# Column sums in four parts, paced weight splits and later value halves in a clustered attention with an MLP behind it

## The chip, the cores and the metric

The kernel runs on one core of one Trainium2 chip. Its time is device microseconds (us) of one execution. The engines are named as in the profile: PE (TensorE, the matmuls), DVE (VectorE), ACT (ScalarE), POOL (GpSimd), and SP, whose queue issues every DMA of this program.

## The reference: clustered attention, then an MLP

Four batches of eight heads, 768 positions, 64 numbers a head. Queries and keys are each assigned to the nearest of 16 centroids of their head; a query sees only the keys of its own cluster. Behind it comes an MLP on the 3072 rows of 512 numbers.

```python
mask = q_assign[:, :, :, None] == k_assign[:, :, None, :]
scores = scale * np.matmul(q, k.transpose(0, 1, 3, 2))
scores = np.where(mask, scores, -1000000000.0)
attn = np.exp(scores - np.max(scores, axis=-1, keepdims=True))
attn = attn / (np.sum(attn, axis=-1, keepdims=True) + 1e-09)
x = np.matmul(attn, v)            # heads side by side: [3072, 512]
h = x @ w_in                      # 512 -> 2048
r = np.maximum(h, 0.0)
g = s * (r * r) + b
out = g @ w_out                   # 2048 -> 512
```

The constant b is added to every element of g, so it reaches the output as b times the column sums of `w_out`. These column sums are one of the things that the change moves.

## The kernel before: units of attention, steps of the MLP, one loop

**Units and steps.** The work is one loop over i (lines 802 to 845). Attention is cut into 192 units: a unit is one head with 128 queries, and in step i unit i gets its scores (`scores`, line 507, four matmuls), its maximum (`maxima`, line 521, DVE) and its exponentials (`exps`, line 528, ACT). The transposed probabilities meet the values four steps later (`value`, line 605, 18 matmuls into the unused columns of a scores bank; the first 16 units go another way, `values`, line 572). Four units make a piece of x (`finish_x`, line 631). The MLP runs `LAG` = 21 steps behind: step m = i - 21 does one of 16 slices ft of the hidden width for 256 rows: `mlp_in` (line 670, 12 matmuls), `mlp_relu` (line 679, three operations on ACT), `mlp_gl` (line 689, POOL), and three steps later `mlp_out` (line 694, 12 matmuls). After the sixteenth slice the two accumulators are scaled, the bias is added (line 711, DVE) and the result is stored.

**Precision.** Most operands are kept as two float16 tiles, a high half (ACT copies the scaled number to float16) and a low half (DVE takes the scaled number minus the high half). `split` (line 216) does this for keys, queries and values, `wsplit` (line 300) for the weights: per slice ft one ACT and one DVE operation for `w_in` (tiles `wis`) and one of each for `w_out` (`wos`). The operation on DVE is a SCALAR_TENSOR_TENSOR with two inputs, line 225 or 310.

**Weights.** The weights arrive as 64 bit floats in 32 DMAs, are packed into float32 by ACT and DVE (`rebase`, `narrow`, lines 242 to 250) and their magnitudes are taken (`bound`, line 252). Only when all 32 are known is the scale in `glob` known (`finish_w_in`, `finish_w_out`), and only then can any weight be split. `wsplit(ft)` is registered at step 17 + ft (line 742). The slices from 4 on are issued behind `first_x`, the two operations that end the fourth piece of x (lines 639 to 641, 306 and 309): from that point nothing holds them back.

**Value halves.** `prep_v(0)` (line 451) splits the four value tiles of the first batch. The first units don't use the halves, only units from 16 on do. It asks for steps 14, 16, 18 and 20 (line 482), but the order of instructions on each engine is not the order of this text: a scheduler orders them by their priority and by when it takes their inputs to be ready. `issue_after`, used through `behind` (line 149), tells it to put an instruction behind another. Nothing of the kind stands at line 490.

**Column sums.** `column_sums` (line 314) is called once, with the last slice of the first MLP chunk (line 709): 32 matmuls with a matrix of ones over all the `wos` halves into one bank, `pb`, and one scaling by DVE into `bias` (line 321).

**Banks.** `small_bank` (line 102) hands out two PSUM banks, h and m, in turn, from step 21 on: the hidden slices of the MLP, the small reductions and `pb` share them.

Of the kernel before, what the change touches and what calls it, by code (L numbers as in the profile page):

```python
# [13 lines left out]
AF = mybir.ActivationFunctionType  # L14
ALU = mybir.AluOpType
# [11 lines left out]
def tile_cluster_attention_mlp(ctx, tc, q, k, v, cent, w_in, w_out, s_in, b_in, out):  # L27
# [47 lines left out]
    last_transpose = [None]  # L75
    first_x = [None, None]
    last_turn = [None]
# [60 lines left out]
    def copy(eng, dst, src):  # L138
        if eng is A:
            A.activation(dst, src, AF.Copy)  # L140
        else:
            eng.tensor_copy(dst, src)

# [156 lines left out]
    def wsplit(ft):  # L300
        while narrowed[0] < 2 * NF:
            next(wgen)
        made = []
        for w, f in ((wi[ft], glob[:, 2:3]), (wo[ft], glob[:, 5:6])):
            e = parts(weight_tile(f"w{'io'[len(made)]}s{ft}"))
            with behind(*first_x[: 2 * (ft >= 4)]):
                A.activation(e[:, 0], w, AF.Copy, scale=f)
            yield
            with behind(*first_x[: 2 * (ft >= 4)]):
                V.scalar_tensor_tensor(e[:, 1], w, f, e[:, 0], op0=ALU.mult, op1=ALU.subtract)  # L310
            made.append(e)
        WSP[ft] = (made[0], made[1].rearrange("p e a f -> p e (a f)"))

    def column_sums():
        pb = small_bank("pb", "m")
        for ft in range(NF):
            for e in range(2):
                nc.tensor.matmul(pb, ones16, WSP[ft][1][:, e, :], start=(ft + e == 0), stop=(ft + e == NF))
        V.tensor_tensor(glob[:, 7:8], bv, glob[:, 4:5], op=ALU.mult)
        bias.append(weight_tile("bias").rearrange("p a f -> p (a f)"))  # L320
        V.tensor_scalar(bias[0], pb, glob[:, 7:8], None, op0=ALU.mult)

# [69 lines left out]
    def prep_q(b, c, hq):  # L392
        n = f"{b}_{c}_{hq}"
        nh = 4
        if b or c > 1:
            qn = sb.tile([P, CT * DM], F32, tag="stage", name=f"qn_{n}", bufs=3)
        else:
            qn = sb.tile([P, T * P], F32, tag="big", name=f"qn_{n}", bufs=BIGN)
# [52 lines left out]
    def prep_v(b):  # L451
# [28 lines left out]
        for hp in range(NP):  # L480
            if b == 0:
                yield from until(RAW - 2 + 2 * hp)
            if b == 1 and hp == 0:
# [5 lines left out]
            G.memset(vh[:, :, :, D:], 1.0)  # L489
            yield from split(vh[:, :, :, :D], vl, vns[hp], vm[:, 7:8], False)  # L490
            if hp < NP - 1:
# [56 lines left out]
    def low(i):  # L548
        u = U[i]
        if i < TURN:  # L550
# [7 lines left out]
            for e in range(2):  # L558
# [3 lines left out]
                if i < RAW:  # L562
                    copy((V, A)[e], flat[:, cols], turned[:, e, : n * P])
                else:
                    A.activation(two[:, 0, cols], turned[:, e, : n * P], AF.Copy)
                    V.tensor_tensor(two[:, 1, cols], turned[:, e, : n * P], two[:, 0, cols], op=ALU.subtract)
# [64 lines left out]
    def finish_x(g):  # L631
# [6 lines left out]
        xn = sb.tile([P, CT, 2, 2, D], F16, tag="xn", name=f"xn_{g}", bufs=1)  # L638
        made = [A.activation(xn[:, :, 0], xs, AF.Copy), absmax(XM[(b, c)][:, hp : hp + 1], xs.rearrange("p t h d -> p (t h d)"))]
        if g == NP - 1:  # L640
            first_x[:] = made
        yield
# [36 lines left out]
    def mlp_relu(b, c, ft):  # L679
        n = f"{b}_{c}_{ft}"  # L680
        ph = GS[(b, c, ft)]
        r = sb.tile([P, CW], F32, tag="r", name=f"r_{n}", bufs=2)
        A.activation(r, ph[:, :CW], AF.Relu, scale=MS[(b, c)][0])  # L683
        g = gs[:, ft % 4]
# [9 lines left out]
    def mlp_out(b, c, ft):  # L694
# [10 lines left out]
        if ft == NF - 1:  # L705
            _, e, acc = MS.pop((b, c))
            o = sb.tile([P, CT, DM], F32, tag="stage", name=f"o_{n}", bufs=3)
            if b + c == 0:
                column_sums()
            for t in range(CT):  # L710
# [30 lines left out]
    for ft in range(NF):  # L741
        at(LAG - 4 + ft, wsplit(ft))
    wgen = weights()

# [127 lines left out]
```

## Time and profile before

| | us |
|---|---|
| median of 3 runs | 911.07 |
| lowest and highest of the runs | 909.8 and 915.86 |
| the profiled execution, its own time | 912.4 |
| its span | 910.7 |
| PE busy in the span | 830.3 (91%) |
| ACT busy | 712.7 (78%) |
| DVE busy | 631.2 (69%) |
| POOL busy | 544.0 (60%) |

An execution's own time and its span differ by 1.7 us, what lies around the program. Busy shares are averages over stages that differ much, so the prediction reads them by stretches of the span. In a group's row the columns are: line, engine, operation, output<-input, count, then busy us and mean ns of one. In the timeline a row gives the start, the duration and, in brackets, how long the engine stood idle ahead of it and what ended that. A row of a table by stretches gives the stretch, its length, for each engine the busy us with the number of instructions, the granted TensorE clock as a share of full speed, and the share and rate of the DMA.

### The profile page before, as it was taken

How to read it: one execution, taken by the hardware profiler on the slowest of the kernel's cores; microseconds unless marked ns; L12 is line 12 of the kernel's file. 1: busy time of each engine (PE TensorE's matmuls, PEld its weight loads, DVE VectorE, ACT ScalarE, POOL GpSimd, SP SyncE). 2: the span in 40 equal slices, each digit the busy share in tenths (PEclk: the TensorE clock that was granted, in tenths of full speed). 3: DMA queues.
4: the chain of work that ended last, by engine and by line, in shares of the span. 5: the costliest groups of instructions: out<-in, count | busy, mean ns of one | idle time of the engine just before them, and what ended most of it. 6: DMA issues, size and time to landing. Idle time of an engine off the chain costs nothing.

```text
span 910.7 us, 22840 instructions
## 1 busy us (share of the span) xinstructions
PE 830.3 (91%) x8625; PEld 591.9 (65%) x8625; DVE 631.2 (69%) x1673; ACT 712.7 (78%) x1406; POOL 544.0 (60%) x580
## 2 busy tenths in 40 slices
PE   1675786899999899999999999999999999999997
PEld 0564664566677667777667767677677777777764
DVE  8789789979778758766877667669777557564200
ACT  4579786867798779889888788988988788788553
POOL 3111024587687668768778667777876667676422
PEclk9977576999999999999999999999999999999999
DMA  5997624697998897989899989689988767676200
GB/s 151 245 287 239 205 49 91 163 178 163 182 181 140 182 209 139 175 158 180 175 180 190 181 152 185 154 150 207 177 156 171 140 124 173 117 149 132 59 24 23
DMA packets 437758, 144.23 MB, mean 158 GB/s; under 512 B 405392, under 2 KB 434064, under 8 KB 437648
## 3 DMA queue, kind: packets, MB, share of 16 engines
q1 hardware_dynamic: 437648, 142.78, 76.1%
q8 instruction: 67, 1.10, 0.5%
q14 instruction: 43, 0.35, 0.1%
HBM read 35.69 MB, written 6.29 MB: 46 GB/s over the span
## 4 chain that ended last, share of the span: by engine, by line
PE 44%; DVE 21%; DMA 14%; ACT 9%; issue 6%; POOL 3%; SPq 2%; DVEq 0%; ACTq 0%; POOLq 0%
PE h L676 15%; PE acc L703 14%; PE sc L516 7%; DMA kn<-in_k_dram 4%; DVE ssm L526 4%; DMA qn<-in_q_dram 4%; ACT p L536 2%; PE sc L617 2%; PE sc L619 2%; ACT ssm L533 2%; PE sc L618 2%; DMA vn<-in_v_dram 2%; DVE ka L225 2%; SPq L570 1%; POOL ph L568 1%
## 5 line engine op out<-in xcount | busy, mean ns | idle before, releaser
L568 POOL TENSOR_TENSOR ph<-p,ph 128x768 f16<-128x768 f32 x176 | 296.3, 1683 | 154.0 <-ACT ph L140 63.9
L676 PE MATMUL h<-xk,wis 128*128 128x256 f16 x2304 | 288.3, 274 | 5.1 <-DMA xk<-xn 2.3
L703 PE MATMUL acc<-wos,gs 128*128 128x512 f16 x1152 | 280.6, 379 | 2.0 <-DVE o L711 0.8
L676 PEld LDWEIGHTS <-wis 128*128 128x128 f16 x2304 | 222.9, 98 | 63.6 <-issue 6.3
L536 ACT ACTIVATE p<-sc,ssm,qsm 128x768 f32<-128x768 f32 x192 | 189.3, 986 | 4.3
L526 DVE TENSOR_REDUCE ssm<-sc 128x1 f32<-128x768 f32 x192 | 181.9, 947 | 6.3 <-PE sc L516 6.2
L691 POOL TENSOR_TENSOR gs<-r,gs 128x256 f16<-128x256 f32 x192 | 136.1, 710 | 64.3 <-ACT r L686 55.3
L703 PEld LDWEIGHTS <-gs 128*128 128x128 f16 x1152 | 104.4, 98 | 94.8 <-issue 1.1
L533 ACT ACTIVATE ssm<-ssm,lift,qsm 128x1 f32<-128x1 f32 x192 | 73.0, 381 | 83.2 <-DVE ssm L526 82.5
L140 ACT ACTIVATE ph<-p 128x768 f16<-128x768 f32 x164 | 137.2, 836 | 0.6
L683 ACT ACTIVATE r<-h,cf 128x256 f32<-128x256 f32 x192 | 89.1, 465 | 39.8 <-PE h L676 34.0
L617 PE MATMUL sc<-halves,PT 128*128 128x65 f16 x1032 | 113.0, 195 | 0.1
L618 PE MATMUL sc<-halves,PT 128*128 128x64 f16 x1032 | 112.9, 192 | 0.0
L619 PE MATMUL sc<-halves,PT 128*128 128x65 f16 x1032 | 112.6, 193 | 0.0
L516 PE MATMUL sc<-keys,QA 128*128 128x384 f16 x384 | 99.8, 341 | 12.8 <-ACT p L536 10.9
L516 PE MATMUL sc<-keys,QB 128*128 128x384 f16 x384 | 99.7, 341 | 8.3 <-DMA QB<-qb 8.3
L617 PEld LDWEIGHTS <-PT 128*128 128x128 f16 x1056 | 99.0, 97 | 11.9 <-DMA PT<-ph 0.8
L618 PEld LDWEIGHTS <-PT 128*128 128x128 f16 x1056 | 98.1, 99 | 11.6 <-issue 0.7
L619 PEld LDWEIGHTS <-PT 128*128 128x128 f16 x1056 | 98.3, 97 | 0.0
L686 ACT ACTIVATE r<-r 128x256 f32<-128x256 f32 x192 | 79.2, 413 | 4.0
L623 DVE TENSOR_SCALAR ssm<-sc 128x1 f32<-128x1 f32 x172 | 26.3, 153 | 80.5 <-PE sc L619 79.0
L685 ACT ACTIVATE gs<-r 128x256 f16<-128x256 f32 x192 | 78.6, 411 | 1.6
(191 smaller groups left out, 1104.7 us busy)
## 6 DMA issues: line engine op xcount, KB each, us to landing
wst<-in_moe_w_in_dram SPq DMA_DIRECT2D x16, 512.0 KB, 4.7
kn<-in_k_dram SPq DMA_DIRECT2D x16, 384.0 KB, 4.2
qn<-in_q_dram SPq DMA_DIRECT2D x24, 256.0 KB, 3.6
vn<-in_v_dram SPq DMA_DIRECT2D x16, 384.0 KB, 3.9
out_dram<-o SPq DMA_DIRECT2D x12, 512.0 KB, 3.3
wst<-in_moe_w_out_dram SPq DMA_DIRECT2D x8, 512.0 KB, 5.0
gs<-in_moe_w_out_dram SPq DMA_DIRECT2D x8, 512.0 KB, 5.8
PT<-ph SPq DMA_TRANSPOSE x176, 3.5
```

What stands on the lines that cost most here:

```text
L140: A.activation(dst, src, AF.Copy)
L516: last_score[0] = nc.tensor.matmul(sc[:, e, :HALF], X[:, col, :], y[:, h * S + e * HALF : h * S + (e + 1) * HALF], start=st, stop=not st)
L526: last_max[0] = V.tensor_reduce(SM[i // 4][:, 0, j : j + 1], U[i]["sc"], axis=AX.XY, op=ALU.max, negate=True)
L533: A.activation(bi, sm[:, 0, j : j + 1], AF.Identity, scale=u["scale"], bias=lift)
L536: last_exp[0] = A.activation(p.rearrange("p (a b) -> p a b", a=2), u["sc"], AF.Exp, bias=bi, scale=u["scale"], **total)
L568: G.tensor_tensor(u["ph"][:, 1, :], u["p"], u["ph"][:, 0, :], op=ALU.subtract)
L617: nc.tensor.matmul(o1, PT[:, kt, :], vh[:, h, kt, : D + 1], start=(kt == 0), stop=False)
L618: nc.tensor.matmul(o, PT[:, kt, :], vl[:, h, kt, :], start=False, stop=False)
L619: nc.tensor.matmul(o1, PT[:, T + kt, :], vh[:, h, kt, : D + 1], start=False, stop=(kt == T - 1))
L676: nc.tensor.matmul(ph[:, :CW], WSP[ft][0][:, wl, kt, :], XS[(b, c, kt)][:, :, xl, :], start=(i == 0), stop=(i == len(terms) - 1))
L691: G.tensor_tensor(g[:, 1, :], r, g[:, 0, :], op=ALU.subtract)
L703: nc.tensor.matmul(acc[:, t, :], g[:, gl, rows], WSP[ft][1][:, wl, :], start=(ft == 0 and gl + wl == 0), stop=(ft == NF - 1 and gl == 1))
```

## The change

Four edits.

1. `column_sums(n)` takes a quarter of the slices, waits until their `wsplit` has been issued, and runs from step 20 + 4n on. Each quarter has a bank of its own (`pb_0` to `pb_3`); the first writes `bias`, the others add to it with a SCALAR_TENSOR_TENSOR on DVE.
2. `wsplit(ft)`: ACT's part of the slices from 4 on is issued behind the newest `Relu` of the MLP, DVE's part behind the newest maximum; slices 1 to 3 behind the last copies of the first 16 units.
3. `prep_v(0)` asks for steps 16, 19, 22 and 25, and both operations of each split are issued behind the newest exponential and the newest maximum.
4. The query tile of chunk 1, second half of the first batch, comes from the three `stage` buffers, which the weights also use, and not from the eleven `big` ones.

```diff
-            with behind(*first_x[: 2 * (ft >= 4)]):
+            with behind(*([last_relu[0]] if ft >= 4 else last_copy if ft else ())):
                 A.activation(e[:, 0], w, AF.Copy, scale=f)
             yield
-            with behind(*first_x[: 2 * (ft >= 4)]):
+            with behind(*([last_max[0]] if ft >= 4 else last_copy if ft else ())):
                 V.scalar_tensor_tensor(e[:, 1], w, f, e[:, 0], op0=ALU.mult, op1=ALU.subtract)
...
-    def column_sums():
-        pb = small_bank("pb", "m")
-        for ft in range(NF):
+    def column_sums(n):
+        q = NF // 4
+        while len(WSP) < (n + 1) * q:
+            yield
+        pb = small_bank(f"pb_{n}", "h")
+        for ft in range(n * q, (n + 1) * q):
             for e in range(2):
-                nc.tensor.matmul(pb, ones16, WSP[ft][1][:, e, :], start=(ft + e == 0), stop=(ft + e == NF))
-        V.tensor_tensor(glob[:, 7:8], bv, glob[:, 4:5], op=ALU.mult)
-        bias.append(weight_tile("bias").rearrange("p a f -> p (a f)"))
-        V.tensor_scalar(bias[0], pb, glob[:, 7:8], None, op0=ALU.mult)
+                nc.tensor.matmul(pb, ones16, WSP[ft][1][:, e, :], start=(ft + e == n * q), stop=(ft + e == (n + 1) * q))
+        if n == 0:
+            V.tensor_tensor(glob[:, 7:8], bv, glob[:, 4:5], op=ALU.mult)
+            bias.append(weight_tile("bias").rearrange("p a f -> p (a f)"))
+            V.tensor_scalar(bias[0], pb, glob[:, 7:8], None, op0=ALU.mult)
+        else:
+            V.scalar_tensor_tensor(bias[0], pb, glob[:, 7:8], bias[0], op0=ALU.mult, op1=ALU.add)
...
-        if b or c > 1:
+        if b or c > 1 or c + hq > 1:
             qn = sb.tile([P, CT * DM], F32, tag="stage", name=f"qn_{n}", bufs=3)
...
             if b == 0:
-                yield from until(RAW - 2 + 2 * hp)
+                yield from until(RAW + 3 * hp)
...
-            yield from split(vh[:, :, :, :D], vl, vns[hp], vm[:, 7:8], False)
+            parted = split(vh[:, :, :, :D], vl, vns[hp], vm[:, 7:8], False)
+            with behind(*((last_exp[0], last_max[0]) if b == 0 else ())):
+                next(parted)
+            yield
+            with behind(*((last_exp[0], last_max[0]) if b == 0 else ())):
+                next(parted, None)
...
-            if b + c == 0:
-                column_sums()
...
+    for n in range(4):
+        at(LAG - 1 + NF // 4 * n, column_sums(n))
```

Three places in the order of the instructions, before and after. Names carry the tile's number; `sc` is a unit's scores bank, `ssm` the tile of its maximum, `wis` and `wos` are split weights, `vn` the values. Line numbers of the changed kernel differ: its maximum is L537 (before L526), its division by the sum L636, L637 and L640 (before L623, L624 and L627).

The first place is DVE in the packing of the weights, before:

```order
L249 SCALAR_TENSOR_TENSOR wi9_835<-wst_18_836,wi9_835 128x512
L225 SCALAR_TENSOR_TENSOR halves_131<-vn_0_0_319,vm_0_318,halves_131 128x768
L225 SCALAR_TENSOR_TENSOR halves_131<-vn_0_1_443,vm_0_318,halves_131 128x768
L262 TENSOR_REDUCE w1_132<-pw_7_826 128x1
L225 SCALAR_TENSOR_TENSOR halves_131<-vn_0_2_511,vm_0_318,halves_131 128x768
L225 SCALAR_TENSOR_TENSOR halves_131<-vn_0_3_588,vm_0_318,halves_131 128x768
L248 TENSOR_SCALAR wo9_843<-wo9_843 128x512
```

All four value halves stood between the packing of weight tiles of slice 9. Now the first of them stands behind the scale of the weights, ahead of the first weight split:

```order
L298 TENSOR_TENSOR glob_134<-sv_252,glob_134 128x1
L225 SCALAR_TENSOR_TENSOR halves_131<-vn_0_0_319,vm_0_318,halves_131 128x768
L421 TENSOR_TENSOR qsm_0_1_1_1259<-qsm_0_1_1_1259,ksm_0_0_151 128x2
L323 TENSOR_TENSOR glob_134<-bv_254,glob_134 128x1
L310 SCALAR_TENSOR_TENSOR wis0_1362<-wi0_246,glob_134,wis0_1362 128x512
```

The second place is DVE from the maximum of unit 20 to that of unit 21, before:

```order
L526 TENSOR_REDUCE ssm_20_1469<-sc_20_1440 128x1
L310 SCALAR_TENSOR_TENSOR wos5_1700<-keys_130,glob_134,wos5_1700 128x512
L225 SCALAR_TENSOR_TENSOR qa_0_1_1_1361<-qn_0_1_1_1222,qsm_0_1_1_1262,qb_0_1_1_1362 128x4x64 x2
L310 SCALAR_TENSOR_TENSOR wis6_1705<-keys_130,glob_134,wis6_1705 128x512
L310 SCALAR_TENSOR_TENSOR wos6_1781<-wo6_684,glob_134,wos6_1781 128x512
L310 SCALAR_TENSOR_TENSOR wis7_1785<-wi7_722,glob_134,wis7_1785 128x512
L623 TENSOR_SCALAR ssm_16_1303<-sc_21_1507 128x1
L310 SCALAR_TENSOR_TENSOR wos7_1863<-wo7_730,glob_134,wos7_1863 128x512
L624 RECIPROCAL ssm_16_1303<-ssm_16_1303 128x1
L310 SCALAR_TENSOR_TENSOR wis8_1865<-wi8_790,glob_134,wis8_1865 128x512
...
L526 TENSOR_REDUCE ssm_20_1469<-sc_21_1507 128x1
```

And after, where the six weight splits have left this place and the second value half has come in; slice 7 is now split six units later:

```order
L537 TENSOR_REDUCE ssm_20_1465<-sc_20_1436 128x1
L225 SCALAR_TENSOR_TENSOR halves_131<-vn_0_1_443,vm_0_318,halves_131 128x768
L636 TENSOR_SCALAR ssm_16_1300<-sc_21_1502 128x1
L637 RECIPROCAL ssm_16_1300<-ssm_16_1300 128x1
L640 TENSOR_SCALAR xs_4_1461<-sc_21_1502,ssm_16_1300 128x64
L537 TENSOR_REDUCE ssm_20_1465<-sc_21_1502 128x1
```

The third place is PE. Before, nineteen column sums stood ahead of the scores of unit 39 and thirteen ahead of those of unit 40; the piece shows the end of the nineteen:

```order
L318 MATMUL pb_2956<-wos8_1939,ones16_97 128x512
L318 LDWEIGHTS ones16_97
L318 MATMUL pb_2956<-wos9_2010,ones16_97 128x512
L516 LDWEIGHTS QA_0_2_0_1929
L516 MATMUL sc_39_2923<-keys_130,QA_0_2_0_1929 128x384
```

After, the first eight stand between the values of unit 18, in the bank of unit 22, and the scores of unit 23; the others stand ahead of the scores of units 28 and 29, of 32 to 34, and of 36 to 38:

```order
L632 MATMUL sc_22_1573<-halves_131,PT_18_1426 128x65
L321 LDWEIGHTS ones16_97
L321 MATMUL pb_0_1629<-wos0_1410,ones16_97 128x512
...
L321 LDWEIGHTS ones16_97
L321 MATMUL pb_0_1629<-wos3_1569,ones16_97 128x512
L527 LDWEIGHTS QA_0_1_0_993
L527 MATMUL sc_23_1650<-keys_130,QA_0_1_0_993 128x384
```

More of the change, by code (lines that the diff above doesn't have):

```diff
@@ L75, in tile_cluster_attention_mlp @@
     last_transpose = [None]
-    first_x = [None, None]
+    last_relu = [None]
+    last_copy = [None, None]
     last_turn = [None]
@@ L139, in copy @@
         if eng is A:
-            A.activation(dst, src, AF.Copy)
-        else:
-            eng.tensor_copy(dst, src)
+            return A.activation(dst, src, AF.Copy)
+        return eng.tensor_copy(dst, src)
     def scalar_in(src, name):
@@ L562, in low @@
                 if i < RAW:
-                    copy((V, A)[e], flat[:, cols], turned[:, e, : n * P])
+                    done = copy((V, A)[e], flat[:, cols], turned[:, e, : n * P])
+                    if i == RAW - 1:
+                        last_copy[e] = done
                 else:
@@ L638, in finish_x @@
         xn = sb.tile([P, CT, 2, 2, D], F16, tag="xn", name=f"xn_{g}", bufs=1)
-        made = [A.activation(xn[:, :, 0], xs, AF.Copy), absmax(XM[(b, c)][:, hp : hp + 1], xs.rearrange("p t h d -> p (t h d)"))]
-        if g == NP - 1:
-            first_x[:] = made
+        A.activation(xn[:, :, 0], xs, AF.Copy)
+        absmax(XM[(b, c)][:, hp : hp + 1], xs.rearrange("p t h d -> p (t h d)"))
         yield
@@ L682, in mlp_relu @@
         r = sb.tile([P, CW], F32, tag="r", name=f"r_{n}", bufs=2)
-        A.activation(r, ph[:, :CW], AF.Relu, scale=MS[(b, c)][0])
+        last_relu[0] = A.activation(r, ph[:, :CW], AF.Relu, scale=MS[(b, c)][0])
         g = gs[:, ft % 4]
```

## The prediction

> **What bounds the kernel now.** I read the page's busy times first, then the busy times by stretches, then who waited for whom between 119 and 243 us, then the timeline of each engine there.
>
> ```profile
> span 910.7 us, 22840 instructions
> PE 830.3 (91%) x8625; PEld 591.9 (65%) x8625; DVE 631.2 (69%) x1673; ACT 712.7 (78%) x1406; POOL 544.0 (60%) x580
> ```
>
> ```profile
> core 0: us, PE busy (x) PEld busy (x) DVE busy (x) ACT busy (x) POOL busy (x), PEclk, DMA share, GB/s
> 119.00:143.00 24.00, 16.81 (x111) 13.34 (x109) 20.89 (x56) 16.67 (x29) 9.10 (x8) 0.74 0.20 44
> 143.00:177.00 34.00, 26.86 (x248) 18.06 (x246) 33.87 (x63) 25.18 (x48) 16.05 (x13) 0.78 0.65 137
> 177.00:226.00 49.00, 45.05 (x516) 30.58 (x517) 41.14 (x116) 35.90 (x73) 36.03 (x37) 1.00 0.81 164
> 226.00:243.00 17.00, 16.85 (x160) 10.63 (x159) 10.71 (x27) 11.52 (x22) 11.91 (x12) 1.00 1.02 199
> sum 124.00, PE 105.58 PEld 72.60 DVE 106.62 ACT 89.27 POOL 73.09; mean PE 26.39 PEld 18.15 DVE 26.65 ACT 22.32 POOL 18.27
> ...
> 243.00:870.00 627.00, 617.67 (x6845) 440.99 (x6843) 423.81 (x1152) 526.18 (x1032) 441.62 (x445) 1.00 0.82 160
> ```
>
> The last row settles most of it: from 243 us on PE is busy 617.67 of 627 us, DVE only 423.81. What the change does to DVE and ACT can't shorten that stretch, so the time is won or lost ahead of it, in how early the loop gets to that saturated state. These are the exponentials of unit 16, of unit 25 and of unit 40:
>
> ```profile
> 119.22 0.99 ACT L536 ACTIVATE p<-sc,ssm,qsm 128x768 f32<-128x768 f32 x1
> ...
> 176.78 0.97 ACT L536 ACTIVATE p<-sc,ssm,qsm 128x768 f32<-128x768 f32 x1
> ...
> 242.75 0.99 ACT L536 ACTIVATE p<-sc,ssm,qsm 128x768 f32<-128x768 f32 x1
> ```
>
> So 24 units take 124 us. Inside, DVE is the limit first: 33.87 of 34 us between 143 and 177, while PE has 26.86 and that at a granted clock of 0.78. PE takes over between 177 and 226.
>
> ```profile
> PE sc L516 <- ACT p L536: 6.5, 4, 4.3
> ACT ssm L533 <- DVE ssm L526: 12.7, 10, 4.0
> ACT wos L307 <- DVE wos L310: 5.0, 6, 2.4
> DVE ssm L623 <- PE sc L619: 5.1, 5, 2.8
> ```
>
> So the chain of the early units is: PE's scores wait for the bank that ACT's exponential frees (6.5 us, once 4.3), ACT waits for DVE's maximum (12.7), and DVE's maximum stands behind weight splits. The last row, DVE waiting for PE, belongs to the later part.
>
> **The change part by part.** First, *the value halves leave the packing of the weights*.
>
> ```profile
> L225 DVE SCALAR_TENSOR_TENSOR halves<-vn,vm,halves 128x768 f16<-128x768 f32 x4 | 3.9, 1014 | 0.0
> ```
>
> ```profile
> 79.97 3.40 ACT L223 ACTIVATE halves<-vn,vm 128x768 f16<-128x768 f32 x4
> ```
>
> ```profile
> 84.35 0.90 PE L560 MATMUL turned<-ident,p 128*128 128x128 f32 x3 [3.59 <-ACT PT L140]
> ```
>
> Four operations on DVE, 3.9 us, and four on ACT, 3.40 us, side by side around 80 to 86 us; PE stood 3.59 us behind ACT's block. Does the packing then end earlier? It does unless the weights' DMAs set its pace:
>
> ```profile
> 79.00:119.00 40.00, 26.94 (x158) 20.31 (x157) 34.02 (x83) 33.37 (x73) 5.43 (x6) 0.62 0.62 185
> ```
>
> ```profile
> ACT wi L244 <- DMA wst<-in_moe_w_in_dram: 1.6, 4, 0.6
> ACT wo L244 <- DMA gs<-in_moe_w_out_dram: 0.9, 1, 0.9
> ```
>
> ACT waits only 2.5 us for weights, DVE is busy 34.02 of 40 us. The gain lies between nothing (the other chains there fill the hole) and 3.9 (all of it); as DVE has 15% of idle time there I take 3.0. Unit 16 then starts 3.0 us earlier.
>
> Second, *the load between unit 16 and unit 40*. The splits of slices 4 to 15 are only moved inside this stretch: by the order, those from slice 7 on go from behind the maxima of units 20 to 26 to behind those of units 26 to 37. The same is true of the 32 column sums, which all lie inside it before and after:
>
> ```profile
> 225.00:243.00 18.00, 7.23 (x32) 3.07 (x32) 1.00 0.96 188
> ```
>
> They cost 7.23 us of PE, at 0.226 us each, in a place where PE is full, and go to places where PE has room, but they aren't removed. New on DVE in this stretch are the value halves, 3.9 us, and three more evictions of a bank into the bias, each like this one:
>
> ```profile
> 238.94 0.74 DVE L321 TENSOR_SCALAR bias<-pb,glob 128x512 f32<-128x512 f32 x1
> ```
>
> 3 x 0.74 = 2.2 us. DVE's load rises from 106.6 to 106.6 + 3.9 + 2.2 = 112.7 us.
>
> To this comes what the splits cost beside POOL. By stretch, the splits alone on DVE:
>
> ```profile
> core 0: us, DVE busy (x), PEclk, DMA share, GB/s
> 119.00:143.00 24.00, 9.15 (x12) 0.74 0.20 44
> 143.00:157.00 14.00, 8.58 (x11) 0.50 0.36 82
> 157.00:179.00 22.00, 11.80 (x11) 0.98 0.87 179
> sum 60.00, DVE 29.53; mean DVE 9.84
> ```
>
> They take 0.76 and 0.78 us each where POOL is little busy and 1.07 where POOL's subtractions have started. The first 8 stay, the 24 that move cost 29.5 - 8 x 0.76 = 23.4 us now and 24 x 1.07 = 25.7 later, so 2.3 more, 115.0 us in all. One split here shows how far this can go:
>
> ```profile
> 162.98 2.06 DVE L310 SCALAR_TENSOR_TENSOR wos<-wo,glob,wos 128x512 f16<-128x512 f32 x1
> ```
>
> The Trainium skill has a rule that speaks against the change (SBUF — State Buffer, section Who interferes with whom): an operation of VectorE with two inputs in SBUF and a GpSimd operation that reads SBUF exclude each other for a whole instruction. The trace agrees, with 0.74 us at best and 2.06 at worst for one shape. By that rule in full each split could wait for a whole subtraction of POOL; the rival called collisions below prices that.
>
> What idle time stays on DVE? Now it is 124 - 106.6 = 17.4 us. The chain from the last x of the first chunk into the MLP stays, since it waits for PE:
>
> ```profile
> 132.33 0.96 DVE L526 TENSOR_REDUCE ssm<-sc 128x1 f32<-128x768 f32 x1 [0.90 <-PE sc L516]
> 136.16 0.29 DVE L116 TENSOR_REDUCE xm<-turned 128x1 f32<-128x128 f32 x1 [1.72 <-PE turned L115]
> 187.88 0.95 DVE L119 TENSOR_REDUCE vm<-vn 128x1 f32<-128x768 f32 x1 [2.03 <-DMA vn<-in_v_dram]
> ```
>
> That is 24 - 20.89 = 3.1 us up to 143 us. The rest lies behind 177 us, 7.9 and 6.3, in waits for PE and for loads like the last row's; there the moved splits now fill DVE. Between 0 and 17.4 I take 5: the 3.1, and 2 of the waits. The stretch becomes 115.0 + 5 = 120 us, 4 less than 124. Its bounds are 112.7 (no idle time, no more collisions), 11.3 less, and 115.0 + 17.4 = 132.4, 8.4 more. ACT's share stays under that: 89.27 us and four value halves of 0.85, 92.7. PE's does too: 105.6 us of which 16.81 and 26.86 ran ahead of 177 us at clocks of 0.74 and 0.78; at full speed these 43.7 would be 33.4, so its floor is 95.
>
> Third, *what is late at unit 40*. In the new order the hidden slice of the second chunk numbered 1 stands behind the scores of unit 41, before it stood amid those of unit 39. PE owes it then:
>
> ```profile
> 184.10 1.47 PE L676 MATMUL h<-xk,wis 128*128 128x256 f16 x12
> ```
>
> Its 12 matmuls take 1.3 us up to the start of the next (185.41). The other MLP work ahead of unit 41 is the same. Bounds 0 and 2.8 (one slice of `acc` more).
>
> *The query tile from a stage buffer* I cost at nothing: in both orders its DMA stands behind the last load of the weights, so none of them waits for it, and it is first needed by unit 24, eight units after its load; a gain or a loss of its own I can't see there. *The waits by issue order* cost nothing by themselves, they only set the order. Behind a split that waits, the next maximum waits on DVE, and ACT's exponential for that; this is the chain above, with one or two splits in it now where there were up to six.
>
> Sum: -3.0 - 4.0 + 1.3 = -5.7 us against the profiled execution's 912.4: 906.7. The median shown is 1.3 below that execution, so **905.5 us**.
>
> ```profile
> DVE 8789789979778758766877667669777557564200
> ```
>
> This row of the page, in tenths of slices of 22.8 us, shows why I don't go further: in the three slices from 182 us on (the ninth to the eleventh) DVE has 7, 9 and 7 already, so there is not much room for what is put there.
>
> **Rivals.** *DVE without gaps.* The waits behind 177 us all vanish, the splits meet POOL no more often than now, and the packing ends 3.9 us earlier: -3.9 - 11.3 + 1.3 = -13.9, so 898.5, by the median 897. For it: DVE did run 33.87 of 34 us when it was the limit, and PE's floor of 95 us allows it. Against it: waits for loads and for PE don't care for the order on DVE.
>
> The Trainium skill (TensorE: Matmul & The Clock Gate, section What's actually happening) says that TensorE falls to half its clock after an idle window of some 3.4 us and comes back after a busy one. The trace agrees with a clock of 0.50 between 143 and 157 us, behind this wait:
>
> ```profile
> 142.55 0.80 PE L516 MATMUL sc<-keys,QA 128*128 128x384 f16 x2 [4.28 <-ACT p L536]
> ```
>
> By the rule, without that wait PE runs these matmuls in about half the time; this only lowers PE's floor and serves this rival, in whose sum it is already.
>
> *Collisions.* The splits beside POOL cost not 1.07 but halfway between the 0.74 and the 2.06 above, 1.4 us: 24 x 1.4 = 33.6 instead of 23.4, so 10.2 more on DVE in place of 2.3. The stretch takes 112.7 + 10.2 + 5 = 127.9: -3.0 + 3.9 + 1.3 = +2.2, by the median 913. For it: POOL is busy 36.03 of 49 us where the splits go, 9.10 and 16.05 of 58 where they come from. Against: only four of the last eleven splits now took over 1.2 us.
>
> *A column sum holds a bank.* Each part keeps one of the two banks of the MLP from its first matmul until DVE has evicted it, and DVE's eviction stands in order behind splits. If the next hidden slice needs that bank, PE, which is in order, stops until then, at worst as long as its longest wait for this chain now, 4.28 us, for each part: 4 x 4.28 = 17.1, less the 5.7: +11.4, by the median 922.5. It decides from the second part on, where 8.6 exceed 5.7. For it: parts 1 to 3 are spread over two or three units each in the order. Against: the hidden slices and the reductions share these banks now, and PE's longest wait for one is short:
>
> ```profile
> PE h L676 <- DVE qsm L116: 1.1, 1, 1.1
> ```
>
> That the change doesn't do what it says is excluded by the order on DVE and PE.
>
> **How the numbers follow.** My forecast gets 0.54, with a range of its own of 900 to 911 and a quarter of its chance under 902; DVE without gaps 0.22, collisions 0.12, the held bank 0.12. One per cent is 9.1 us, about what a measurement of this kernel can tell from no change. Faster by more: 0.22 + 0.14 = 0.36. Slower by more: 0.12. Within: 0.52. The range leaves out the held bank and a little below the second case: 894 to 917.
>
> **What would show it.** Right: the scale of the weights known 3 us earlier; unit 25's exponential (now at 176.8 us) about 10 us earlier, and most of it paid back by unit 37; the idle 4.28 us of PE and the clock of 0.50 gone; the column sums spread out; splits at 1.0 to 1.1 us; from unit 40 on everything as before. Wrong: DVE's idle time between units 16 and 40 far from 5 us, splits at 1.4 us, or PE waiting for a bias eviction.

## The result and the profile after

The changed kernel takes 916.67 us (median of 17 runs, 912.43 to 922.88); the kernel before takes 912.57 us beside it (17 runs, 908.38 to 915.86). The ratio, which compares all the runs, is 1.0058, 95% interval 1.0041 to 1.0075: some 5 us slower, where 5.7 us faster were forecast. The two medians alone lie 4.1 us apart. A second measurement (`change_again` below) gives 1.0048.

The page of the changed kernel, its first lines:

```profile
span 914.1 us, 22817 instructions
...
PE 829.2 (91%) x8625; PEld 587.7 (64%) x8625; DVE 633.2 (69%) x1676; ACT 710.7 (78%) x1406; POOL 546.7 (60%) x580
```

PE has no more work than before (8625 matmuls in both, busy for 829.2 and 830.3 us), yet the span is 3.4 us longer: PE stands idle more. Where? First the same three exponentials as in the prediction, units 16, 25 and 40:

```profile
113.82 0.98 ACT L547 ACTIVATE p<-sc,ssm,qsm 128x768 f32<-128x768 f32 x1
...
162.59 0.99 ACT L547 ACTIVATE p<-sc,ssm,qsm 128x768 f32<-128x768 f32 x1
...
238.51 0.99 ACT L547 ACTIVATE p<-sc,ssm,qsm 128x768 f32<-128x768 f32 x1
```

They come 5.4, 14.2 and 4.2 us earlier than before, so up to unit 40 the change did gain. The busy times from unit 16 to 25, 25 to 37 and 37 to 40 (the first split in two) show how most of unit 25's lead was paid back:

```profile
core 0: us, PE busy (x) PEld busy (x) DVE busy (x) ACT busy (x) POOL busy (x), PEclk, DMA share, GB/s
113.80:137.60 23.80, 17.94 (x144) 13.80 (x144) 21.56 (x61) 14.60 (x25) 10.07 (x10) 0.74 0.30 67
137.60:162.60 25.00, 23.06 (x209) 15.18 (x208) 19.61 (x35) 17.17 (x35) 15.51 (x13) 0.91 0.67 135
162.60:222.45 59.85, 48.63 (x505) 31.37 (x505) 58.52 (x131) 47.54 (x89) 37.27 (x33) 1.00 0.65 145
222.45:238.50 16.05, 11.54 (x157) 8.59 (x155) 13.27 (x35) 10.19 (x18) 11.39 (x12) 0.98 0.92 201
sum 124.70, PE 101.17 PEld 68.94 DVE 112.96 ACT 89.51 POOL 74.24; mean PE 25.29 PEld 17.24 DVE 28.24 ACT 22.38 POOL 18.56
```

Between units 25 and 37 DVE is busy 58.52 of 59.85 us: the splits put there have filled it.

And then the later units. Times compare only at units that have the same PE work ahead of their scores in both kernels. The start of a unit's scores on PE then says how far PE has come (at unit 40 the change still owes one hidden slice, some 1.3 us):

| unit | scores start before, us | after, us | after minus before |
|---|---|---|---|
| 40 (one slice owed) | 237.16 | 230.30 | -6.9 |
| 47 | 266.56 | 265.50 | -1.1 |
| 60 | 320.59 | 317.28 | -3.3 |
| 78 | 392.37 | 392.41 | 0.0 |
| 108 | 512.61 | 511.04 | -1.6 |
| 112 | 528.53 | 528.01 | -0.5 |
| 122 | 569.68 | 572.86 | +3.2 |
| 191 | 840.98 | 844.38 | +3.4 |

So at unit 40 PE is ahead about as far as forecast (7.0 us), and the lead is lost behind it, in three places: between units 40 and 47, between 60 and 78, and between 108 and 122. (In between some of it comes back.) The first place is just behind the stretch that the forecast reckoned:

```profile
235.70 0.69 DVE L120 TENSOR_REDUCE amb_q<-qn 128x2 bf16<-128x512 f32 x1 [1.86 <-DMA qn<-in_q_dram]
...
236.60 0.47 ACT L695 ACTIVATE r<-h,cf 128x256 f32<-128x256 f32 x1 [2.47 <-DVE cf L677]
...
237.12 2.11 PE L688 MATMUL h<-xk,wis 128*128 128x256 f16 x12 [2.14 <-ACT r L695]
...
238.00:242.00 4.00, 4.00 (x16) 2.00 (x15) 1.68 (x7) 3.60 (x9) 2.24 (x3) 0.60 0.76 162
```

DVE stands 1.86 us in front of a query tile that is still loading. Behind it in DVE's order stands the factor `cf`, for which ACT's Relu waits, and PE waits 2.14 us for the Relu. Then the granted clock is 0.60 in the mean from 238 to 242 us, where it was 1.00 before. Of the 5.8 us that go up to unit 47, 1.3 are the owed slice and 2.1 this wait; the lower clock is some 1.6 more, estimated as 0.40 of 4 us.

The exponentials of units 60, 74, 108 and 111 show the other two places, before and after (these four have the same PE work ahead as well):

```profile
326.80 0.99 ACT L536 ACTIVATE p<-sc,ssm,qsm 128x768 f32<-128x768 f32 x1
...
381.61 0.99 ACT L536 ACTIVATE p<-sc,ssm,qsm 128x768 f32<-128x768 f32 x1
...
517.20 0.99 ACT L536 ACTIVATE p<-sc,ssm,qsm 128x768 f32<-128x768 f32 x1
...
530.48 0.99 ACT L536 ACTIVATE p<-sc,ssm,qsm 128x768 f32<-128x768 f32 x1
```

```profile
321.73 0.99 ACT L547 ACTIVATE p<-sc,ssm,qsm 128x768 f32<-128x768 f32 x1
...
382.38 0.99 ACT L547 ACTIVATE p<-sc,ssm,qsm 128x768 f32<-128x768 f32 x1
...
515.53 0.99 ACT L547 ACTIVATE p<-sc,ssm,qsm 128x768 f32<-128x768 f32 x1
...
533.24 0.98 ACT L547 ACTIVATE p<-sc,ssm,qsm 128x768 f32<-128x768 f32 x1
```

After minus before is -5.1, +0.8, -1.7 and +2.8 us, and +3.4 at the last unit. An exponential also waits for its own maximum on DVE, so it moves more than PE's scores. The -5.1 is -3.3 by the scores: in the kernel before, the exponential of unit 60 is held up by a wait of DVE. And of the 4.4 us that the exponentials lose between units 108 and 111, the scores have lost 1.1 by unit 112; the other 3.7 that they lose follow by unit 122.

What happens at units 108 to 111 stands in DVE's timeline, before and after. L119 and L120 are the same line, `absmax`; `vm<-vn` takes the maximum of a value tile of the last batch:

```profile
514.35 0.95 DVE L119 TENSOR_REDUCE vm<-vn 128x1 f32<-128x768 f32 x1 [2.28 <-DMA vn<-in_v_dram]
...
520.64 0.95 DVE L119 TENSOR_REDUCE vm<-vn 128x1 f32<-128x768 f32 x1 [3.35 <-DMA vn<-in_v_dram]
...
523.96 0.95 DVE L119 TENSOR_REDUCE vm<-vn 128x1 f32<-128x768 f32 x1 [0.53 <-DMA vn<-in_v_dram]
...
526.48 0.94 DVE L119 TENSOR_REDUCE vm<-vn 128x1 f32<-128x768 f32 x1
```

```profile
519.32 0.95 DVE L120 TENSOR_REDUCE vm<-vn 128x1 f32<-128x768 f32 x1 [4.25 <-DMA vn<-in_v_dram]
...
530.15 0.95 DVE L120 TENSOR_REDUCE vm<-vn 128x1 f32<-128x768 f32 x1 [4.76 <-DMA vn<-in_v_dram]
531.02 0.15 DVE L636 TENSOR_SCALAR ssm<-sc 128x1 f32<-128x1 f32 x1
...
531.40 0.29 DVE L640 TENSOR_SCALAR xs<-sc,ssm 128x64 f32<-128x64 f32 x1
531.60 0.95 DVE L537 TENSOR_REDUCE ssm<-sc 128x1 f32<-128x768 f32 x1
```

DVE works in order and stands 4.25 and 4.76 us in front of a tile that is still loading, and behind it stand the division by the sum and the next unit's maximum, which ACT and PE need. The last tile is late because its load is. SP's queue, from the third load of these tiles to the fourth, before and after:

```profile
520.10 0.58 SPq L91 DMA_DIRECT2D vn<-in_v_dram  x1
521.10 1.49 SPq L570 DMA_TRANSPOSE PT<-ph  x1
522.64 0.58 SPq L91 DMA_DIRECT2D vn<-in_v_dram  x1
```

```profile
519.14 0.58 SPq L92 DMA_DIRECT2D vn<-in_v_dram  x1
522.96 1.41 SPq L583 DMA_TRANSPOSE PT<-ph  x1
524.48 1.34 SPq L450 DMA_TRANSPOSE QB<-qb  x1
525.88 0.57 SPq L92 DMA_DIRECT2D vn<-in_v_dram  x1
```

Before, one transpose stands between the third and the fourth load; after, two, and POOL makes what they move, by the subtraction for `ph` and the mask for `qb`:

```profile
520.88 0.46 POOL L338 TENSOR_TENSOR oe_q<-oe_q,rev 128x128 f32<-128x128 f32 x1 [4.89 <-DVE ssm L636]
521.29 1.64 POOL L581 TENSOR_TENSOR ph<-p,ph 128x768 f16<-128x768 f32 x1
...
523.58 0.62 POOL L341 TENSOR_SCALAR qb<-oo_q 128x512 f16<-128x512 f16 x1
```

The first transpose leaves at 522.96, when `ph` is made (522.93), 3.2 us after the third load has gone out; the second follows it. POOL itself had stood idle 4.89 us for DVE, which stood in front of an earlier value tile until 519.32. So it is a ring: a late load holds up DVE, DVE holds up POOL, POOL the transposes, and these the next load in SP's queue. That load goes out 6.7 us after the one ahead of it, not 2.5, and its tile is taken up 4.3 us later. The Trainium skill (DMA: Bandwidth & Descriptors, section Anatomy of one DMA) says that the DMA engines don't wait on semaphores, that every such wait happens on the sequencer that issues; the trace agrees: the value load at 525.88 leaves only when the transposes ahead of it have left.

### The profile page after: what moved, and what is told of

Read it like the earlier page. It is cut to its first block, busy times and chain, and to the rows that moved or that the text cites. A ratio compares the mean times of both kernels' runs of the same rounds, so it can differ in the third digit from the quotient of the medians.

```text
span 914.1 us, 22817 instructions
## 1 busy us (share of the span) xinstructions
PE 829.2 (91%) x8625; PEld 587.7 (64%) x8625; DVE 633.2 (69%) x1676; ACT 710.7 (78%) x1406; POOL 546.7 (60%) x580
## 5 line engine op out<-in xcount | busy, mean ns | idle before, releaser
L715 PE MATMUL acc<-wos,gs 128*128 128x512 f16 x1152 | 284.6, 380 | 4.8 <-POOL gs L703 2.6
L537 DVE TENSOR_REDUCE ssm<-sc 128x1 f32<-128x768 f32 x192 | 182.0, 948 | 2.4 <-PE sc L527 2.2
L636 DVE TENSOR_SCALAR ssm<-sc 128x1 f32<-128x1 f32 x172 | 26.3, 153 | 87.4 <-PE sc L632 86.6
```

Source lines behind the costliest of these rows:

```text
L537: last_max[0] = V.tensor_reduce(SM[i // 4][:, 0, j : j + 1], U[i]["sc"], axis=AX.XY, op=ALU.max, negate=True)
L715: nc.tensor.matmul(acc[:, t, :], g[:, gl, rows], WSP[ft][1][:, wl, :], start=(ft == 0 and gl + wl == 0), stop=(ft == NF - 1 and gl == 1))
```

## The experiments

Theories, formed from these rows. LATE or LOADS: the loss comes from the later order, at last from DVE standing in front of late value loads. EARLY: it comes from the splits and halves crowded into units 16 to 43. BANKS: from the column sums' banks. SEQUENCE: from the order of PE's own blocks at units 108 to 111. (Compared place by place, PE's order from the scores of unit 107 to those of unit 112 is the same in both kernels, which alone speaks against SEQUENCE there; from 112 to 121 it differs.)

### Which edit?

The scheduler gives each set of edits an order, and for the first four runs these fall into two kinds from unit 78 on: that of the kernel before, and that of the change. That separates the theories better than the edits do.

`sums_only` is the kernel before with edit 1, `halves_only` with edit 3, `sums_and_halves` with both; `no_halves` is the change with edit 3 taken back:

```diff
-                yield from until(RAW + 3 * hp)
+                yield from until(RAW - 2 + 2 * hp)
...
-            parted = split(vh[:, :, :, :D], vl, vns[hp], vm[:, 7:8], False)
...
+            yield from split(vh[:, :, :, :D], vl, vns[hp], vm[:, 7:8], False)
```

> The kernel before with edit 1 alone: column sums in four parts, each with its own bank and DVE eviction. In its order of instructions PE does units 78 to 121 as the whole change does, not as the kernel before. Theory LATE (the loss comes from that order, after unit 100; the profile of the whole change loses 4.4 us between the exponentials of units 100 and 118): slower by 3 to 6 us, ratio 1.004 to 1.006, and the loss between units 100 and 118. Theory EARLY (the loss comes from the DVE load of moved splits and halves before unit 43, and nothing is lost later): within 1.5 us, ratio 1.000. Theory BANKS (parts of the sums hold a bank, PE waits for their evictions): slower by 3 to 6 us, lost before unit 100.

> The kernel before with edit 3 alone: value halves at steps 16 to 25 behind the exponentials and maxima. PE does units 78 to 121 in the order of the whole change. LATE: unit 16 about 5 us earlier, yet 2 to 5 us slower in the end, ratio 1.002 to 1.006. EARLY: with the splits at their old place the lead is not paid back, 2 to 5 us faster, ratio 0.995 to 0.998. BANKS: not slower, 0.995 to 1.000.

> The kernel before with edits 1 and 3, splits as before. PE does everything from unit 74 on in the order of the kernel before. LATE: 0 to 3 us faster, ratio 0.997 to 1.000, no loss between units 100 and 118. EARLY: 2 to 5 us faster, 0.995 to 0.998. BANKS: slower by 2 to 5 us, 1.002 to 1.006.

> The whole change without edit 3: value halves at their old steps, sums in parts, paced splits, stage tile. PE does everything from unit 59 on in the order of the kernel before. LATE: within 2 us, ratio 0.997 to 1.002, no loss between units 100 and 118. EARLY: unit 16 without its lead and the paced splits still there, slower by 4 to 8 us, 1.004 to 1.009. BANKS: slower by 4 to 6 us, 1.004 to 1.007.

Measured; the last column is how much longer than in the kernel before the profile has it from unit 108's exponential to unit 111's:

| kernel | order of units 78 to 121 | ratio to before (95%) | 108 to 111: us longer |
|---|---|---|---|
| the change | change | 1.0058 (1.0041 to 1.0075) | +4.4 |
| `sums_only` | change | 1.0023 (1.0000 to 1.0047) | +3.1 |
| `halves_only` | change | 1.0087 (1.0063 to 1.0111) | +3.8 |
| `sums_and_halves` | before | 1.0009 (0.9989 to 1.0029) | +0.2 |
| `no_halves` | before | 0.9982 (0.9961 to 1.0003) | -0.2 |

EARLY falls: `halves_only`, which it had faster, is the slowest, and `no_halves`, with the paced splits and without the early lead, isn't slower. BANKS falls with `no_halves` too. The loss at units 108 to 111 goes with the order, as LATE has it. In size LATE missed: `sums_only` is 0.0023 slower and not 0.004, `sums_and_halves` is not faster, and by PE's scores `halves_only` lost 5.1 us and `sums_and_halves` 6.6 between units 64 and 72; why there was not tried.

Two more of this kind ran later. `change_again` is the change, unaltered; `splits_as_before` is the change without edit 2:

```diff
-            with behind(*([last_relu[0]] if ft >= 4 else last_copy if ft else ())):
+            with behind(*first_x[: 2 * (ft >= 4)]):
                 A.activation(e[:, 0], w, AF.Copy, scale=f)
             yield
-            with behind(*([last_max[0]] if ft >= 4 else last_copy if ft else ())):
+            with behind(*first_x[: 2 * (ft >= 4)]):
```

> The whole change once more, beside the others on one chip: 1.004 to 1.007 by its first measurement. Its loss in the profile should lie at the same two places, units 60 to 74 and 108 to 111, by every theory that puts it down to the order.

> The whole change without edit 2: the splits of slices 4 to 15 behind the last x of the first chunk, as before. It has an order of its own up to unit 155. LOADS: its time is set by the same kind of waits at units 60 to 74 and 108 to 111, so 1.000 to 1.008, which one can't be told from the edit. EARLY (the paced splits cost what is lost): 0.995 to 0.998.

They gave 1.0048 (1.0027 to 1.0070), with both later losses in place (from -5.1 to +1.3 us between units 60 and 74, from +1.4 to +5.0 between 108 and 111), and 1.0087 (1.0059 to 1.0115). Without paced splits the change is not faster but slower, against EARLY again. Its later order is its own, but already at unit 49, with the same PE work ahead, its scores are 5.0 us behind the kernel before, the change's 1.1 ahead: the paced splits gain early.

### Value maxima out of the way

`late_values_3` puts the four maxima of the last batch's value tiles behind those of units 116 to 119; `late_values_23` does it for the last two batches (`b > 1`). `before_late_values_3` and `before_late_values_23` are the same in the kernel before:

```diff
-            absmax(vm[:, hp : hp + 1], vns[hp].rearrange("p h t d -> p (h t d)"))
+            with behind(last_max[0] if b > 2 else None):
+                absmax(vm[:, hp : hp + 1], vns[hp].rearrange("p h t d -> p (h t d)"))
```

> The whole change, and the four maxima of the value tiles of the last batch put behind the maxima of units 116 to 119 instead of 107 to 110, when their loads have long landed. PE's order is the change's up to unit 112. Theory LOADS (the 4.4 us between units 108 and 111 are lost because DVE, in order, stands 4.25 and 4.76 us in front of a value tile that is still loading, and what PE waits for stands behind it): 3 to 4.4 us faster than the whole change, ratio to the kernel before 1.001 to 1.003, the loss between units 108 and 111 gone. Theory SEQUENCE (it is lost by the order of PE's own blocks, which stays): no change there, ratio 1.005 to 1.006, units 108 to 111 still lose 4.

> The same for the last two batches (maxima behind those of units 68 to 71 instead of 60 to 62, too). The whole change loses 4.4 us between units 60 and 65, where DVE waits for value loads as well. LOADS: another 2 to 4 us, ratio to the kernel before 0.996 to 1.000. SEQUENCE: 1.005 to 1.006.

> The kernel before, with the maxima of the last batch's value tiles behind those of units 116 to 119. LOADS: before, PE had 1.3 us of idle time there, so up to 1.3 us faster, ratio 0.998 to 1.000. SEQUENCE: 1.000.

> The kernel before, with the maxima of the last two batches' value tiles moved. LOADS: PE had 0.6 us of idle time at units 60 to 65 in the kernel before, so 0 to 2 us faster, ratio 0.998 to 1.000. SEQUENCE: 1.000.

`late_values_3`: 1.0002 (0.9978 to 1.0026). Units 108 and 111 in its profile:

```profile
519.64 0.99 ACT L548 ACTIVATE p<-sc,ssm,qsm 128x768 f32<-128x768 f32 x1
...
531.06 0.99 ACT L548 ACTIVATE p<-sc,ssm,qsm 128x768 f32<-128x768 f32 x1
```

Three units in 11.42 us, where the change takes 17.71 and the kernel before 13.28, though PE's order up to unit 112 is the change's in every place. So at these units it is not SEQUENCE: what cost was DVE in front of the late tile. From unit 112 to 118 PE's order in this kernel is that of the kernel before, so for the 3.7 us that the change's scores lose there the loads and the order are not parted; 1.6 of them are one wait of PE for the eviction of the accumulators (at 566.29 us). The profiled execution of `late_values_3` is one of its longer ones, 917.25 us with a median of 913.36, and in it 2.2 us go between units 78 and 108 already. `late_values_23`: 1.0016 (0.9995 to 1.0037); here LOADS missed. By PE's scores nothing is lost between units 60 and 68 (4.2 and 4.7 us ahead; the change 3.3 and 1.1), but 3.8 go by unit 79, in another order of PE, with a wait for the query tile's transpose and a granted clock of 0.66 from 355 to 360 us:

```profile
355.92 0.20 PE L446 MATMUL pq<-cT,QA 128*128 128x16 f16 x1 [2.25 <-DMA QA<-qa]
```

The kernels before: 1.0005 (0.9977 to 1.0032) and 0.9974 (0.9954 to 0.9994); the second gained a little, about as far as LOADS allowed.

### Loads ahead of their use

`loads_ahead` keeps the late value maxima (`b > 1`) and treats the query tiles likewise, loaded a step earlier, their maximum a step later. `before_loads_ahead` is the same in the kernel before, `queries_ahead` the query part alone in the change:

```diff
-        absmax(qm, qn.rearrange("p (j h) t d -> p j (h t d)", j=2))
+        if b:
+            yield
+        with behind(last_max[0] if b else None):
+            absmax(qm, qn.rearrange("p (j h) t d -> p j (h t d)", j=2))
...
-                    at(s0, prep_q(b, c, hq))
+                    at(s0 - (b > 0), prep_q(b, c, hq))
```

> The whole change with the loads of batches 1 to 3 no longer late: value maxima of the last two batches behind the maxima of units 68 to 71 and 116 to 119, query tiles loaded one step earlier and their maximum behind the newest one. Theory LOADS: DVE's waits for loads of values and queries (44 us in the whole change from 243 us on) fall under 15, the lead of 4 to 5 us that the MLP's slices show up to 342 us stays to the end, ratio to the kernel before 0.993 to 0.998. If the lead is gone by unit 74 all the same, something else than late loads takes it there: 0.999 to 1.003.

> The kernel before with the same moves. LOADS: PE waited 4.4 us for the query tile's transposes and little for DVE, so 1 to 4 us faster, ratio 0.996 to 0.999, and the whole change with the same moves 3 to 5 us ahead of it. If late loads don't matter: 1.000, and both the same.

> The whole change with the query loads alone moved: one step earlier, their maximum behind the newest one; value tiles as in the change. LATE LOAD: the loss between units 60 and 74 shrinks by 2 to 3 us, the one at units 108 to 111 stays, ratio 1.000 to 1.004. If the queries carry all of it: 0.995 to 0.998. If the value tiles do: 1.004 to 1.007.

`loads_ahead`: 0.9947 (0.9926 to 0.9967), 907.5 us, faster than both kernels. DVE's waits for values and queries from 243 us on fell from 44.5 to 14.6 us. `before_loads_ahead`: 0.9992 (0.9975 to 1.0008). With loads ahead in both, the change is 0.0045 ahead, 4.1 us; but PE's order differs between the two up to unit 161, so this is not the edits' alone. `queries_ahead`: 1.0062 (1.0040 to 1.0085), slower than LATE LOAD had it; in an order of its own from unit 48 to 161 the queries gain nothing alone.

`splits_as_before_ahead` and `no_halves_ahead` are `loads_ahead` without edit 2 and without edit 3 (the diffs above):

> The kernel with all loads ahead, without edit 2: splits behind the last x of the first chunk. Same order from unit 55 on as with edit 2, so the difference is edit 2 alone. Expected from the leads at unit 43 of runs with and without paced splits, a lead 3 to 6 us smaller than with edit 2: ratio to the kernel before 0.998 to 1.002. If paced splits give nothing that lasts: 0.994 to 0.996, as with them.

> The kernel with all loads ahead, without edit 3: value halves at their old steps. Same order from unit 62 on as the kernel before with loads ahead (0.9992). If the lead is the value halves' (unit 16 is 5 us earlier with them alone): 0.998 to 1.001, as before. If it is the paced splits': 0.994 to 0.997.

They gave 1.0011 (0.9990 to 1.0031) and 0.9983 (0.9965 to 1.0002). The first has the order of `loads_ahead` from unit 58 on, so edit 2 is worth 1.0011 - 0.9947 = 0.0064, 5.8 us, to the other edits. The second has the order of `before_loads_ahead` (0.9992) from unit 62 on: without the halves the other edits give nothing that can be measured. So the paced splits gain, and only with the later halves. What the halves themselves gain can't be told here: the order changes with them up to unit 161.

### Or only the value loads, earlier

`values_loaded_early` leaves the value maxima of the last two batches where the change has them and issues the loads four steps earlier; `values_loaded_2_early` two steps; `before_values_early` is the kernel before with four steps, its maxima pinned at its own places, and PE's order unchanged throughout. `every_max` lists the units' maxima:

```diff
-            absmax(vm[:, hp : hp + 1], vns[hp].rearrange("p h t d -> p (h t d)"))
+            with behind(every_max[{2: (60, 60, 61, 62), 3: (107, 108, 109, 110)}[b][hp]] if b > 1 else None):
+                absmax(vm[:, hp : hp + 1], vns[hp].rearrange("p h t d -> p (h t d)"))
...
-            at(START[b][1], prep_v(b))
+            at(START[b][1] - 4 * (b > 1), prep_v(b))
```

> The whole change with the value tiles of the last two batches loaded four steps earlier, their maxima kept at the same places (behind the maxima of units 60 to 62 and 107 to 110). Theory LATE LOAD: DVE's waits of 4.25 and 4.76 us for value tiles go, the loss between units 108 and 111 goes with them (under 1.5 us), ratio to the kernel before 0.999 to 1.003. Theory PLACE (the maxima cost by standing there, loaded or not): 1.004 to 1.007, and the loss of 4.4 us stays.

> The whole change with the value tiles of the last two batches loaded two steps (some 9 us) earlier, their maxima where they are; PE's order between units 62 and 107 is neither the change's nor that of the kernel before. LATE LOAD: the waits of up to 4.8 us are covered by two steps, so 0.994 to 0.998 again. If the order was what helped: anywhere between 0.998 and 1.007.

> The kernel before with the value tiles of the last two batches loaded four steps earlier, their maxima where they are; PE's order is that of the kernel before in every place. LATE LOAD: before, DVE waits 13.9 us for value tiles but PE only 1 to 2 us behind them, so ratio 0.998 to 1.000, and 3 to 5 us of the 0.9953 belong to the change. If early loads alone are worth it: 0.994 to 0.997.

`values_loaded_early`: 0.9953 (0.9931 to 0.9976). `values_loaded_2_early`: 0.9925 (0.9901 to 0.9949), 907.2 us, the best of all. `before_values_early`: 0.9966 (0.9947 to 0.9985), more than LATE LOAD gave the kernel before; as PE's order is the same in every place, these 3.1 us (1.4 to 4.8 by the interval) are what the late value loads cost it. From unit 68 on `values_loaded_early` has this order too. With early value loads in both, the change is then 0.0013 ahead, 1.2 us, which the intervals don't tell from nothing. What held up DVE from 243 to 870 us, in the change and in `values_loaded_2_early` (us in total, times, longest; the second and third row of each list, the first is a wait for PE):

```profile
DVE amb_q L120 <- DMA qn<-in_q_dram: 26.2, 14, 3.9
DVE vm L120 <- DMA vn<-in_v_dram: 18.3, 7, 4.8
```

```profile
DVE amb_q L121 <- DMA qn<-in_q_dram: 30.4, 15, 3.7
DVE om_q L336 <- PE pq L448: 15.2, 14, 1.9
```

The wait for `vn` is gone, the one for `qn` has grown, and the kernel is faster by 0.013 than the change and no slower than `loads_ahead`, whose DVE waits least for loads: it isn't the sum of DVE's waiting that counts but what stands behind a wait. Units 60, 108 and 111 and the last one:

```profile
319.72 0.99 ACT L550 ACTIVATE p<-sc,ssm,qsm 128x768 f32<-128x768 f32 x1
...
512.83 0.99 ACT L550 ACTIVATE p<-sc,ssm,qsm 128x768 f32<-128x768 f32 x1
...
524.05 0.99 ACT L550 ACTIVATE p<-sc,ssm,qsm 128x768 f32<-128x768 f32 x1
...
837.59 0.99 ACT L550 ACTIVATE p<-sc,ssm,qsm 128x768 f32<-128x768 f32 x1
```

They are 7.1 us ahead of the kernel before at unit 60, 4.4 at 108, 6.4 at 111 and 6.8 at the end: between 108 and 111 nothing is lost now. By PE's scores the lead is 5.5 us at unit 60, 3.1 at 78, 5.8 at 122 and 6.8 at the end, so behind unit 60 a part is still lost. `values_loaded_early` keeps it there: 4.4 and 3.9.

What stays open: in `values_loaded_early` PE's order from unit 68 on is that of the kernel before, and in the other it is a third one, so the loads' share and the order's are not fully apart there; only at units 108 to 111, and over the whole kernel before, are they. No run has the change's order of units 112 to 121, where it loses most of that, without the late value tiles. The loss between units 60 and 78 came back in `late_values_23` as a wait for another load's chain; that it can be kept away is shown by `values_loaded_early`, not that the value tiles alone cause it. The wait at unit 41 is in the trace of the change and of `change_again` (1.44 us of PE there) and gone in that of `loads_ahead`; what it costs in the end was not measured.

## Why the prediction was wrong, by its own steps

**What bounds the kernel.** "So the time is won or lost ahead of it" is the step that failed, and with it "from unit 40 on everything as before". PE busy 617.67 of 627 us was read as a part that hands a lead on whole. It isn't: the change reorders the units up to 121, and PE's idle time there grew, at units 41 and 108 to 111 behind DVE in front of late loads. By PE's scores the change was 6.9 us ahead at unit 40 with 1.3 owed, the forecast's sum; at unit 47 1.1 ahead, at the last 3.4 behind. By stretches, before and after:

```profile
320.00:345.00 25.00, 24.32 (x275) 16.81 (x274) 15.18 (x41) 19.46 (x38) 15.57 (x17) 1.00 0.95 190
...
480.00:545.00 65.00, 63.59 (x688) 44.84 (x685) 42.98 (x119) 53.24 (x105) 44.42 (x46) 1.00 0.95 177
```

```profile
320.00:345.00 25.00, 22.41 (x244) 15.50 (x242) 14.10 (x42) 17.80 (x36) 15.21 (x15) 1.00 0.85 189
...
480.00:545.00 65.00, 61.02 (x664) 42.58 (x663) 45.66 (x116) 50.88 (x102) 41.96 (x44) 1.00 0.83 175
```

PE loses 1.9 and 2.6 us more than before in these two. The row of the prediction itself left 9.3 us in which PE is idle, more than the whole forecast: in the change they are 11.9 (busy 615.10 of 627), in `before_values_early` 7.2 (619.81), which is 3.1 us faster (0.0034 of 911). The Trainium skill (Perfetto Trace Analysis, the note ahead of its first section) says, of judging how close a kernel comes to the chip's peak, that matmul busy time is a bad metric, because matmuls are pipelined; no run here tests that.

**Halves out of the packing**, -3.0 in bounds of 0 to 3.9: mis-sized. The first split of a weight on ACT starts at 117.52 us, before at 123.20, and unit 16 is 5.4 us earlier. `halves_only` has 4.7 at unit 16, so it is this edit. Up to 1.2 us of both are the execution: four kernels with PE's early order unchanged have unit 16 at 118.0 to 118.8 us. The bound counted DVE's 3.9 us and left out that PE's wait of 3.59 us behind ACT's block shrinks as well, to 0.99; that this is the rest is not shown.

**Units 16 to 40**, -4.0: the load was right, 112.96 us of DVE where 112.7 to 115.0 were reckoned, with splits at 0.97 us in the late stretch and not 1.07. The idle time was not: 124.70 - 112.96 = 11.7 us instead of 5. The stretch took 124.70 us and gave nothing; 5.4 of the idle lie between 137.6 and 162.6 us, where DVE has 19.61 of 25.00. The forecast's "unit 25 about 10 us earlier, mostly paid back by unit 37" came as 14.2 and 3.7. The 4.28 us of idle PE are gone (its longest wait up to unit 40 is 2.1). The clock of 0.50 is gone between 143 and 157 us, below; it is not gone altogether, with 0.91 from 137.6 to 162.6 us and 0.60 from 238 to 242:

```profile
143.00:157.00 14.00, 12.41 (x127) 8.47 (x126) 11.30 (x20) 12.01 (x26) 7.79 (x7) 1.00 0.75 170
```

The two errors cancel in part at unit 40: its exponential is 4.2 us earlier, its scores 6.9, where 7.0 were forecast.

**Late at unit 40**, +1.3: by count, one slice (12 hidden matmuls) was owed there, as said.

**Query tile at nothing**: not tried by itself.

**Rivals.** A column sum that holds a bank: PE waited for splits (3.2 us) at the sums, never for a bias eviction, and `no_halves` speaks against it. Collisions: splits at 0.97 us. DVE without gaps: 11.7 us of gaps. The way it went, a lead lost again at later loads, was not among them.

What the mechanism of the forecast is worth without late loads stays open, with 5.7 us as its sum: `loads_ahead` against `before_loads_ahead` gives 4.1, in different orders, `values_loaded_early` against `before_values_early` 1.2, in the same order from unit 68 on.

That 916.67 us lie just inside the stated range of 894 to 917 is luck: its upper part was there for collisions, which did not come.

## What to carry to other kernels

A stretch in which the first engine is 98% busy hands on a lead only as long as the order in it and what it waits for stay; its remaining idle time can be more than the change is worth. Where a scheduler reorders it, compare two points with the same work ahead of them on that engine, and look for operations on an in-order engine that stand in front of a load. Give such loads some steps of distance before judging a change further up: here four steps were worth 0.0034 to the kernel before, in an unchanged order of PE, and with two the changed kernel came out 0.0133 faster, its order having changed too. Test an edit against a kernel with the same later order, or what the order does is taken for the edit.

## What was not expected of the hardware

A value load of 384 KB went out 6.7 us after the one ahead of it: a transpose in the same queue waited 3.2 us for POOL, and the issuing of it and of a second one took 2.8; another 4.3 us passed until DVE could use the tile. And one wait of PE of 2.14 us, at unit 41, was followed by a granted clock of 0.60 over four us.
